# Local and pooled attention with two feed-forward layers: three stages, weights decoded into place, 512-token blocks

## The chip, the cores and the metric

One core of a Trainium2 chip runs the whole program. The time is the device time of one execution in microseconds (us). Data lies in SBUF and matmul results in PSUM (8 banks); TensorE (PE) multiplies, VectorE (DVE), ScalarE (ACT) and GpSimd (POOL) do the elementwise work, and DMA queues of SyncE (SP) and ScalarE move data to and from DRAM.

## The reference

```python
# q, k, v: [4, 8, 576, 64]; pooled attention over means of 4 tokens, repeated 4 times
out_d = sm_attn(mean4(q), mean4(k), mean4(v))           # 144 queries, 144 keys
# local attention: |i - j| < 4
scores = where(mask, 0.125 * q @ k.T, -1e9); out_local = softmax(scores) @ v
x = (repeat(out_d, 4) + out_local) -> [2304, 512]       # tokens, heads * dim
x = ((x @ w_a) * (x @ w_b)) @ w_out                     # 512 -> 1536 -> 512
h = x @ w_in; return (h * clip(h + 3, 0, 6) / 6) @ w_out2   # 512 -> 2048 -> 512
```

The weights arrive as float64. Every matrix product of the two feed-forward layers is done in three passes on operands split into two float32r parts (small terms first, `PASSES`).

## The kernel before, in words

Attention works on units of 116 tokens (5 to a batch, 20 in all; the last of a batch has 112). `local` does half a unit, two head pairs: scores against keys laid out with zeros (`kz`, L306), maximum, exponentials, scaling, a transpose (`turn`) and the product with the values (`pv`), which adds the pooled result and splits the sum into `x`. `pooled` does one head pair of one batch (16 in all): sums over four tokens, 144 x 144 scores, softmax, product.

Weights are decoded by `decode` (L83 to L124): a load of 1 MB into `raw`, five VectorE passes (L102, L103, L104, L107, L109) that turn float64 words into float32, an add (L115, on GpSimd) and a split into two parts (`split`, L79 on ScalarE, L80). The 12 tiles of `wab` go to their places (`wh`). The 6 tiles of `wo` and the 16 of `w2` are written to DRAM (`later_weights`) and read back at the last block (L542, L547).

The first feed-forward layer's hidden part is done in six blocks of 3, 3 and 4 units (348, 344 and 460 tokens), 12 tiles each (`pab`, L523), and stored to DRAM (`h_d`). In the last part, blocks of 256 tokens run `second` (acc, L569) for the next block between `ph` (L601) and `last` (oacc, L591) of the present one.

The order is written as lists of (time, task) in slots of half a tile; a `tick` in the projection loop issues what is due. The compiler's planner then orders each engine's instructions by the order of the program and its own estimate of when operands are ready. An engine takes its instructions in order, and so do the SP and ACT DMA queues.

Of the kernel before, what the change touches and what calls it, by code (L numbers as in the profile page):

```python
# [25 lines left out]
UW = QB + KB             # tokens that a unit sees  # L26
# [5 lines left out]
HL = 2                   # tiles of the hidden layer in a load  # L32
HP = 4                   # head pairs
SCALE = 0.125

# The upper words, read as float32, of the least and the largest weight that float32r holds.
# [3 lines left out]
# (part of the weights, part of the activations): small terms first  # L40
# [3 lines left out]
PAR = {'banks': 1, 'b_draw': 3, 'dec': 'pp pp pv', 'b_eT': 2, 'abufs': 3, 'b_dq': 1, 'b_e': 4, 'early': -5, 'ord0': 4, 'b_dk': 1, 'lead': 3, 'pem': '111', 'ld0': 2, 'means': 'pv pv vv', 'spl': 'vvp', 'th0': 0.5, 'ls2': 2, 'every0': 3, 'cl': 'pppvvv', 'at0': 3, 'tail': 3, 'b_z': 4, 'th1': 1, 'b_dv': 1, 'norm': 'va ap pp', 'm1': 4, 'th2': 1, 'every': 1.7, 'ahead': 3, 'pre': 5, 'cp': 'aa aa aa', 'vs': 'ppp', 'step0': 2.5, 'lead2': 2, 'ahead0': 2, 'b_vraw': 1, 'hq': 'a', 'nab': 4, 'tk': 1, 'nlast': 5, 'b_de': 3, 'b_mx': 2, 'b_xf': 2, 'b_q': 2, 'mexp': '000'}  # L44


@with_exitstack
def fused_kernel(ctx: ExitStack, tc: tile.TileContext, qt, kt, vt, qd, kd, vd, wab, wo, w2, mask, out):
# [9 lines left out]
    wpool = ctx.enter_context(tc.tile_pool(name="wpool", bufs=1))  # L58
    dram = ctx.enter_context(tc.tile_pool(name="dram", bufs=1, space=bass.MemoryType.DRAM))
    ps = ctx.enter_context(tc.tile_pool(name="ps", bufs=1, space=PSUM))  # L60

# [5 lines left out]
    nc.sync.dma_start(mask_sb, mask)  # L67
# [5 lines left out]
    w2_d = dram.tile([F2, P, 2, W], F32, name="w2_d")  # L73
    wo_d = dram.tile([F1 // 2, P, 2, W], F32, name="wo_d")
    h_d = dram.tile([F1, P, NT], F32, name="h_d")

    def split(dst, src, eng):
        """dst[:, 0] + dst[:, 1] == src, each part with 12 significant bits."""
        nc.scalar.activation(dst[:, 0], src, AF.Copy)  # L79
        eng.tensor_tensor(dst[:, 1], src, dst[:, 0], op=ALU.subtract)  # L80

    def decode(pool, src, dst, put=None, add=nc.gpsimd, sub=nc.gpsimd):
        """float64 -> float32, rounded to nearest, in two parts: [load, first part, second part, put]  # L83

        dst(raw) gives tiles [P, 2, n] with n adding up to W, in order."""
        T = {}

        def load():
            T["raw"] = pool.tile([P, W], mybir.dt.uint64, tag="raw", bufs=2, name="raw")
            nc.sync.dma_start(T["raw"], src)  # L90

        def words():
            w = T["raw"].bitcast(U32).rearrange("p (n t) -> p n t", t=2)
            return w[:, :, 0], w[:, :, 1]

        def upper():
            lo, hi = words()
            m = T["m"] = pool.tile([P, W], F32, tag="dm", bufs=2, name="m")
# [5 lines left out]
            nc.vector.scalar_tensor_tensor(out=mu, in0=hi, scalar=0xC0000000, in1=mu,  # L104
                                           op0=ALU.bitwise_and, op1=ALU.bitwise_or)
            # the lower word, on the value's binade
            nc.vector.tensor_scalar(hi, mu, 0xFF800000, None, op0=ALU.bitwise_and)  # L107
            low = lo.bitcast(F32)
            nc.vector.scalar_tensor_tensor(out=low, in0=lo, scalar=2.0 ** -52, in1=hi.bitcast(F32),  # L109
                                           op0=ALU.mult, op1=ALU.mult)  # L110

        def parts():
            lo, _ = words()
            m = T["m"]
            add.tensor_tensor(m, m, lo.bitcast(F32), op=ALU.add)  # L115
            T["dst"] = dst(T["raw"])
            at = 0
            for t in T["dst"]:
                n = t.shape[2]
                split(t, m[:, at:at + n], sub)  # L120
                at += n

        return [load, upper, parts, lambda: put(T["dst"])]

    eng = {"a": "act", "p": nc.gpsimd, "v": nc.vector}
    A = PAR.get
    eng = {"a": "act", "p": nc.gpsimd, "v": nc.vector}
    NORM = [[eng[x] for x in y] for y in A("norm", "aa ap pp").split()]
    MEANS = [[eng[x] for x in y] for y in A("means", "pv pv vv").split()]
    PEM = [x == "1" for x in A("pem", "110")]  # L130
    SPL = [eng[x] for x in A("spl", "ppp")]
    VS = [eng[x] for x in A("vs", "ppp")]
    MEXP = [x == "1" for x in A("mexp", "000")]
    CP = A("cp", "aa aa aa").split()
    CL = [eng[x] for x in A("cl", "pppppv")]
    DEC = [[eng[x] for x in y] for y in A("dec", "pp pp pp").split()]
    STEP, AHEAD, TAIL = A("step", 3.3), A("ahead", 3), A("tail", 2)
    AHEAD0, AT0, EVERY0, PRE = A("ahead0", 3), A("at0", 3), A("every0", 3), A("pre", 3)
    EVERY, FIRST, LEAD, LEAD2 = A("every", 1.6), A("first", 0), A("lead", 3), A("lead2", 4)
    EARLY, ABUFS = A("early", -3), A("abufs", 3)  # L140
    BUFS = {"draw": 3, "vraw": 1, "dq": 1, "dk": 1, "dv": 1, "de": 3, "deT": 3, "dmx": 2, "dz": 4, "od": HP,
            "q": 2, "v": 2, "e": 4, "eT": 3, "xf": 1, "mx": 2, "z": 4}
    for x in BUFS:
        BUFS[x] = A("b_" + x, BUFS[x])

# [4 lines left out]
    place, sizes = {}, []    # of a unit: its block and where it begins there; tokens of a block  # L150
    for m in range(B // 2 * len(NBU)):
        sizes.append(0)
        for _ in range(NBU[m % len(NBU)]):
            u = len(place)
            place[u] = m, sizes[m]
            sizes[m] += unit_tokens(u)
    NBLK = len(sizes)
    begin = [sum(sizes[:m]) for m in range(NBLK)]

    ods = {}  # L160
    xs = {}
    loaded = {}

    class Work:
        """Where a part of the attention has its tiles, and which engines do what."""

        def __init__(self, bufs, tags, kz, vz, norm, means, pemask, spl, vs, mexp, cp):
            self.bufs, self.tags, self.kz, self.vz = bufs, tags, kz, vz
            self.norm, self.dnorm = norm
            self.qsum, self.ksum = means  # L170
            self.pemask, self.spl, self.vs, self.mexp, self.cp = pemask, spl, vs, mexp, cp
            self.n = 0

        def tile(self, shape, tag):
            if isinstance(self.bufs[tag], list):
                t = self.bufs[tag].pop(0)
                self.bufs[tag].append(t)
                names = "abc"[:len(shape) - 1]
                sizes = dict(zip(names, shape[1:]))
                return t[:shape[0]].rearrange(f"p ({' '.join(names)}) -> p {' '.join(names)}", **sizes)  # L180
            pool, n = self.bufs[tag]
            return pool.tile(shape, F32, tag=tag, bufs=n, name=tag)

        def psum(self, shape, name):
            tag, n = self.tags[self.n % len(self.tags)]
            self.n += 1
            return ps.tile(shape, F32, tag=tag, bufs=n, name=name)

    def copy(eng, dst, src):
        if eng == "a":  # L190
            nc.scalar.activation(dst, src, AF.Copy)
        else:
            nc.vector.tensor_copy(dst, src)

    def normalise(eng, e, z, n):
        """e[:, i] *= z[:, i], i < n"""
        if eng == "act":
            for i in range(n):
                nc.scalar.activation(e[:, i], e[:, i], AF.Copy, scale=z[:, i:i + 1])
# [488 lines left out]
```

## Time and profile before

| | |
|---|---|
| median of 3 runs | 1084.3 us (1083.38 to 1085.85) |
| profiled execution, first to last instruction | 1085.6 us |
| TensorE matmuls busy | 1017.6 us, 94% |
| VectorE busy | 576.5 us, 53% |
| ScalarE busy | 421.7 us, 39% |
| GpSimd busy | 245.5 us, 23% |
| DMA | 145.42 MB |

Busy shares are averages over very different stages; the slices and stretches below show which engine fills which stage. The program's first and last instructions bound the span, and no other time of the profiled execution is recorded beside it.

### The profile page before, as it was taken

Reading aid. Unit: us, or ns where it says so; the run is one execution under the profiler, and the core shown is the slowest. Engines: PE = TensorE matmul, PEld = TensorE weight load, DVE = VectorE, ACT = ScalarE, POOL = GpSimd, SP = SyncE. Lnnn points to the kernel's source line nnn. Section 1 sums busy time; section 2 is a strip of 40 time slices with the busy share of each in tenths; the row PEclk is TensorE's granted clock in tenths of the full one; section 3 lists DMA queues with packets and bytes.
Section 4 is the critical chain, followed back from the end, with each engine's and each line's share of the span. In section 5 each row is a group of like instructions: output and inputs, shape, how many; then the busy total and the mean of one; then the engine's idle time right before and its main releaser. Section 6 shows DMA issues by size and latency. Waiting matters only on the chain.

```text
span 1085.6 us, 18160 instructions
## 1 busy us (share of the span) xinstructions
PE 1017.6 (94%) x7080; PEld 917.6 (85%) x7080; DVE 576.5 (53%) x1073; ACT 421.7 (39%) x1208; POOL 245.5 (23%) x188
## 2 busy tenths in 40 slices
PE   3668778999999999999999999999999999999998
PEld 2457657987788799999999999999999999999997
DVE  5999998778898887511233323232333333333232
ACT  4643554444544454311233324242333333333242
POOL 4767664344554734300000000000000000000000
PEclk9999968999999999999999999999999999999999
DMA  9835465777777576596641111111011111101000
GB/s 245 228 113 190 153 208 161 237 260 256 260 258 253 207 269 233 197 408 216 219 189 30 40 31 38 34 35 37 23 49 30 40 30 40 30 21 49 1 21 19
DMA packets 54340, 145.42 MB, mean 134 GB/s; under 512 B 6000, under 2 KB 34160, under 8 KB 44272
## 3 DMA queue, kind: packets, MB, share of 16 engines
q1 hardware_dynamic: 39568, 130.13, 35.4%
q10 hardware_dynamic: 14688, 14.16, 4.5%
q8 instruction: 55, 0.90, 0.3%
q14 instruction: 29, 0.24, 0.1%
HBM read 102.32 MB, written 41.94 MB: 133 GB/s over the span
## 4 chain that ended last, share of the span: by engine, by line
PE 71%; DVE 14%; DMA 8%; issue 3%; ACT 2%; POOL 1%; SPq 0%; ACTq 0%; DVEq 0%; POOLq 0%
PE ph L601 19%; PE oacc L591 18%; PE pab L523 16%; PE acc L569 14%; DVE m L104 2%; DVE raw L107 2%; DMA raw<-w 2%; DVE mx L329 1%; PE sc L206 1%; DVE raw L109 1%; DVE m L102 1%; DVE z L338 1%; DMA raw<-wab 1%; DMA raw<-wo 1%; PE po L206 1%
## 5 line engine op out<-in xcount | busy, mean ns | idle before, releaser
L523 PE MATMUL pab<-x,wh 128*128 128x348 f32 (+2 forms) x1728 | 344.6, 353 | 6.8 <-ACT x L79 3.9
L523 PEld LDWEIGHTS pab<-x,wh 128*128 128x128 f32 x1728 | 300.0, 197 | 28.1 <-issue 8.0
L605 DVE SCALAR_TENSOR_TENSOR r<-r,ph 128x256 f32<-128x256 f32 x144 | 60.7, 421 | 293.9 <-ACT r L604 293.1
L604 ACT ACTIVATE r<-ph,three 128x256 f32<-128x256 f32 x144 | 68.4, 475 | 283.2 <-PE ph L601 282.8
L601 PEld LDWEIGHTS ph<-x,wh 128*128 128x128 f32 x1296 | 169.5, 191 | 8.1
L569 PE MATMUL acc<-h,wo 128*128 128x256 f32 x1296 | 175.6, 283 | 0.0
L601 PE MATMUL ph<-x,wh 128*128 128x256 f32 x1296 | 173.4, 283 | 0.0
L591 PE MATMUL oacc<-wh,g 128*128 128x512 f32 x648 | 167.6, 394 | 0.0
L569 PEld LDWEIGHTS acc<-h,wo 128*128 128x128 f32 x1296 | 165.7, 191 | 0.9
L591 PEld LDWEIGHTS oacc<-wh,g 128*128 128x128 f32 x648 | 114.8, 189 | 18.9
L80 DVE TENSOR_TENSOR g<-r,g 128x256 fp32r<-128x256 f32 x144 | 61.2, 425 | 64.2 <-PE acc L569 35.8
L115 POOL TENSOR_TENSOR m<-m,raw 128x1024 f32<-128x1024 f32 x34 | 83.1, 2445 | 47.0 <-issue 14.0
L79 ACT ACTIVATE g<-r 128x256 fp32r<-128x256 f32 x144 | 59.9, 416 | 60.1 <-DVE r L605 60.1
L528 DVE TENSOR_TENSOR a<-a,pab 128x348 f32<-128x348 f32 (+2 forms) x72 | 39.4, 548 | 53.8 <-PE pab L523 32.5
L336 ACT ACTIVATE e<-sc,mx 128x64 f32<-128x64 f32 x136 | 40.9, 315 | 63.5 <-DVE mx L329 56.1
L80 DVE TENSOR_TENSOR h<-hr,h 128x256 fp32r<-128x256 f32 x108 | 45.8, 425 | 33.5 <-ACT h L79 29.4
L601 PEld LDWEIGHTS ph<-x,w 128*128 128x128 f32 x432 | 56.7, 188 | 3.3
L79 ACT ACTIVATE h<-hr 128x256 fp32r<-128x256 f32 x108 | 44.9, 417 | 33.9 <-PE acc L569 26.8
L601 PE MATMUL ph<-x,w 128*128 128x256 f32 x432 | 57.5, 281 | 0.0
L527 ACT ACTIVATE a<-pab 128x348 f32<-128x348 f32 (+2 forms) x72 | 35.4, 491 | 54.3 <-PE pab L523 53.4
L591 PE MATMUL oacc<-w,g 128*128 128x512 f32 x216 | 54.6, 396 | 0.0
L101 ACT ACTIVATE m<-raw 128x1024 f32<-128x1024 f32 x34 | 39.1, 1151 | 30.5 <-DMA raw<-wab 11.2
(89 smaller groups left out, 1051.4 us busy)
## 6 DMA issues: line engine op xcount, KB each, us to landing
raw<-w SPq DMA_DIRECT2D x16, 1024.0 KB
w_d<-raw SPq DMA_DIRECT2D x16, 1024.0 KB, 3.9
hr<-h_d ACTq DMA_DIRECT2D x54, 256.0 KB, 5.5
raw<-wab SPq DMA_DIRECT2D x12, 1024.0 KB, 4.9
wh<-w_d SPq DMA_DIRECT2D x12, 1024.0 KB, 5.4
raw<-wo SPq DMA_DIRECT2D x6, 1024.0 KB
wo_d<-raw SPq DMA_DIRECT2D x6, 1024.0 KB
wo<-wo_d SPq DMA_DIRECT2D x6, 1024.0 KB
```

The source lines that it names most:

```text
L79: nc.scalar.activation(dst[:, 0], src, AF.Copy)
L80: eng.tensor_tensor(dst[:, 1], src, dst[:, 0], op=ALU.subtract)
L101: nc.scalar.activation(m, hi.bitcast(F32), AF.Abs)
L115: add.tensor_tensor(m, m, lo.bitcast(F32), op=ALU.add)
L336: nc.scalar.activation(e[:, i], masked[:, i], AF.Exp, bias=mx[:, i:i + 1], scale=SCALE, accum_out=z[:, i:i + 1])
L523: nc.tensor.matmul(p_, wab_t[f][:, x, c], xs[n, g // 2][:, g % 2, y, :nb], start=(g == 0 and i == 0), stop=(g == KC - 1 and i == 2))
L528: nc.vector.tensor_tensor(a, a, pab[1], op=ALU.mult)
L569: nc.tensor.matmul(accs[n][e], wo_t[f // 2][:, x, c], hs[n, f][:, y], start=(f == 0 and i == 0), stop=(f == F1 - 1 and i == 2))
L591: nc.tensor.matmul(oacc[e], g_[:, x, e * P:(e + 1) * P], w2_t[f][:, y, DM:], start=(f == 0 and i == 0), stop=(f == F2 - 1 and i == 2))
L601: nc.tensor.matmul(ph, w2_t[f][:, x, g * P:(g + 1) * P], x2s[n, g][:, y], start=(g == 0 and i == 0), stop=(g == KC - 1 and i == 2))
L604: nc.scalar.activation(r, ph, AF.Relu, bias=three)
L605: nc.vector.scalar_tensor_tensor(out=r, in0=r, scalar=6.0, in1=ph, op0=ALU.min, op1=ALU.mult)
```

## The change

The program becomes three stages in sequence: hidden part of the first layer (`job`), its second product (`second`, result x2 to DRAM and back), the second layer (`final`). `second` and `final` use 512-token blocks (four, and one of 256). Blocks of attention and projections are of 3, 2, 3, 3, 3, 3, 3 units, and the first jobs go over blocks 0 and 1 with the first six weight tiles, then tiles 6 to 8 of both, and so on. Weights are decoded on VectorE alone, straight into the place where they are used: `wo` during the last projection block, `w2` during `second` in the slots that `wab` leaves. A local step does all four head pairs of a unit at once, a pooled step all four score tiles; q and k are loaded once per head pair of a batch and serve both kinds of attention. Scores share one pair of PSUM banks (`s2`), but in the first two blocks, which also use the projections' banks.

```diff
-NBU = (3, 3, 4)          # units of a block of the first FFN's hidden layer, over two batches
-NC = 256                 # tokens of a block of what follows
+BLOCKS = (3, 2, 3, 3, 3, 3, 3)
+NC = 512
...
+        def rest():          # decode, all of it after the load
...
+            nc.vector.scalar_tensor_tensor(out=low, in0=lo, scalar=2.0 ** -52, in1=m, op0=ALU.mult, op1=ALU.mult)
+            v = hi.bitcast(F32)
+            nc.vector.tensor_tensor(v, v, low, op=ALU.add)
+            w = put()
+            nc.scalar.activation(w[:, 0], v, AF.Copy)
+            nc.vector.tensor_tensor(w[:, 1], v, w[:, 0], op=ALU.subtract)
...
+    def two_banks(first, name):
+        tag = "s2"
+        if first:
+            tag = start_banks[count[0] % len(start_banks)]      # ["s2", "ab", "ab"]
+            count[0] += 1
+        return ps.tile([P, 2, BANK], F32, tag=tag, bufs=2 if tag == "ab" else 1, name=name)
...
+            src = qks[b, g] = ap.tile([P, 2, WQ], F32, tag="qk", bufs=6, name="qk")
...
+            T["v_"] = ap.tile([HD, 2, FACTOR, P], F32, tag="vraw", bufs=1, name="vraw")
...
+                for i, h in ((0, 0), (1, 1), (0, 1), (1, 0)):      # local scores
+                    nc.tensor.matmul(sc[64 * i:64 * i + 64, h, p * KB:(p + 1) * KB],
+                                     src[r, 0, HALO + c:HALO + c + KB], src[r, 1, c:c + KB],
+                                     start=False, stop=(p == HP - 1))
...
+            scaled(nc.vector if first else nc.gpsimd, e.rearrange("q p h k -> q (p h) k"),
+                   z.rearrange("q p h -> q (p h)"))
...
+    def load_h(n, f):
+        h = hs[n, f] = pools["p2"].tile([P, 2, NC], F32R, tag="hg", bufs=4, name="h")[:, :, :hi - lo]
+        nc.scalar.dma_start(h[:, 1].bitcast(F32), h_d[f][:, lo:hi])
+    def split_h(n, f):
+        nc.scalar.activation(h[:, 0], src, AF.Copy)
+        nc.vector.tensor_tensor(h[:, 1], src, h[:, 0], op=ALU.subtract)
...
+    jobs = [(0, f) for f in range(6)] + [(1, f) for f in range(6)]
+    jobs += [(n, f) for f in range(6, 9) for n in range(2)]
+    jobs += [(2, f) for f in range(9)]
+    jobs += [(n, f) for n in range(3) for f in range(9, F1)]
+    jobs += [(n, f) for n in range(3, NBLK) for f in range(F1)]
...
+    attend([([], *x[1:]) for x in g0], -20, -10, 2.5, 0)
+    attend(groups_of(1, True), 0.5, 2, 1.0, 12)
+    attend(groups_of(2), 6, 13, 1.5, 4)
+    attend(groups_of(3), 22, 31, 2.0, 6)
...
+    at = {f: f - 3 for f in range(6)} | {6: 7, 7: 8.5, 8: 10, 9: 16, 10: 19, 11: 22}
+        put(at[f] - 4 if f > 1 else -84 + f, load)      # wab
+        put(at[f], rest)
...
+        put(T1 + 1.8 * i, load)                         # wo; T1: first job of the last block
+        put(T1 + 1.8 * i + 1, rest)
...
+        put(T2 + k - 3, load_h, n, f)                   # T2: number of jobs
+        put(T2 + k - 1.5, split_h, n, f)
+        put(T2 + k, second, n, f)
...
+        t = T2 + 0.5 + 3.6 * f if f < F1 + 2 else T3 + 0.5 + 1.5 * (f - F1 - 2)     # w2
+        put(t - 3, load)
+        put(t, rest)
```

## Rows read from the trace of the kernel before

**Rows 1.** The page, busy tenths in 40 slices of 27 us.

```profile
PE   3668778999999999999999999999999999999998
DVE  5999998778898887511233323232333333333232
```

**Rows 2.** Stretches: us, busy (x) of PE, PEld, DVE, ACT, POOL, clock, DMA, GB/s.

```profile
0.00:69.70 69.70, 32.73 (x252) 22.56 (x252) 57.59 (x105) 34.89 (x129) 41.69 (x42) 1.00 0.76 212
69.70:185.00 115.30, 94.21 (x624) 81.63 (x625) 111.47 (x146) 54.77 (x179) 75.49 (x42) 0.87 0.51 165
185.00:455.00 270.00, 263.80 (x1993) 230.71 (x1992) 219.17 (x376) 132.19 (x439) 127.66 (x103) 0.98 0.70 244
...
540.00:1082.00 542.00, 541.85 (x3717) 503.69 (x3715) 171.88 (x413) 185.14 (x431) 0.00 (x0) 1.00 0.13 40
```

**Rows 3.** The chain that ended last: start us, us, what; matmuls in unbroken runs.

```profile
415.23 3.97 PE pab L523 x24
...
495.71 2.51 PE pab L523 x12
...
656.08 1.44 PE ph L601 x12
657.52 2.80 PE oacc L591 x12
```

**Rows 4.** Timeline of PE, attention at full clock: start us, us, what.

```profile
237.79 0.72 PE L206 MATMUL dsc<-dk,dq 64*72 64x144 f32 x8
...
243.97 0.66 PE L209 MATMUL dpt<-ident,de 72*72 72x72 f32 x8
...
258.63 0.71 PE L206 MATMUL dpo<-deT,dv 72*64 72x144 f32 x8
...
429.33 0.38 PE L209 MATMUL pt<-ident,e 128*128 128x128 f32 x2
...
435.30 0.68 PE L206 MATMUL po<-eT,vz 128*64 128x58 f32 x16
...
439.80 0.28 PE L206 MATMUL sc<-mask_sb,ident 128*128 128x256 bf16 x1
440.01 0.66 PE L206 MATMUL sc<-kz,q 128*64 128x128 f32 x8
```

**Rows 5.** Timeline of DVE, passes of a decode and a small one between.

```profile
401.09 1.21 DVE L80 TENSOR_TENSOR raw<-m,raw 128x1024 fp32r<-128x1024 f32 x1
402.23 0.68 DVE L102 TENSOR_SCALAR m<-m 128x1024 f32<-128x1024 f32 x1
...
403.84 0.16 DVE L329 TENSOR_SCALAR mx<-mx 128x4 f32<-128x4 f32 x1
403.91 1.21 DVE L104 SCALAR_TENSOR_TENSOR m<-raw,m 128x1024 uint32<-128x1024 uint32 x1
...
406.26 1.22 DVE L109 SCALAR_TENSOR_TENSOR raw<-raw 128x1024 f32<-128x1024 uint32 x1
```

**Rows 6.** Lines of VectorE, a small scaling: xcount | busy us, mean ns | idle before.

```profile
L329 DVE TENSOR_SCALAR mx<-mx 128x4 f32<-128x4 f32 x40 | 32.8, 822 | 0.3
```

**Rows 7.** The same view, sums and maxima of attention.

```profile
L327 DVE TENSOR_REDUCE mx<-sc 128x4 f32<-128x256 f32 x40 | 16.5, 413 | 4.2 <-PE sc L206 4.1
...
L225 DVE TENSOR_REDUCE dk<-draw 128x144 f32<-128x576 f32 x12 | 8.9, 738 | 0.0
```

**Rows 8.** The chain that ended last, at the start.

```profile
9.03 10.10 DMA wh<-qd
```

**Rows 9.** Timeline of PE, the first projection; brackets: idle before, and its releaser.

```profile
69.66 1.24 PE L523 MATMUL pab<-x,wh 128*128 128x348 f32 x3 [3.93 <-ACT x L79]
```

**Rows 10.** DMA issues: count, size, median us from issue to landing.

```profile
hr<-h_d ACTq DMA_DIRECT2D x54, 256.0 KB, 5.5
...
out<-o SPq DMA_DIRECT2D x18, 256.0 KB, 2.0
```

**Rows 11.** Lines of VectorE, the split of a hidden tile.

```profile
L80 DVE TENSOR_TENSOR h<-hr,h 128x256 fp32r<-128x256 f32 x108 | 45.8, 425 | 33.5 <-ACT h L79 29.4
```

More of the change, by code (lines that the diff above doesn't have):

```diff
@@ L134, in fused_kernel @@
[L134 to L142, printed above, removed]
@@ L156, in fused_kernel @@
             sizes[m] += unit_tokens(u)
+    begin = [sum(sizes[:m]) for m in range(len(sizes))]
     NBLK = len(sizes)
[L158 to L199, printed above, removed]
-        else:
-            eng.tensor_tensor(e, e, z.unsqueeze(2).to_broadcast(list(e.shape)), op=ALU.mult)
-    newest = [None]
-    def mm(*args, **kw):
-        newest[0] = nc.tensor.matmul(*args, **kw)
@@ L557, in split_h @@
[L557 to L565 removed]
+            dst = xs[m][:, :, :, at:at + tokens]
+            nc.scalar.activation(dst[:, :, 0], xf[:, :, :tokens], AF.Copy)
@@ new lines, in final, with put @@
+        return hidden, last, end
+    events = []
+    def put(t, task, *args):
+        events.append((t, len(events), task, args))
+    jobs = [(0, f) for f in range(6)] + [(1, f) for f in range(6)]
[3 more added lines that the diff above has]
+    jobs += [(n, f) for n in range(3, NBLK) for f in range(F1)]
+    when = {j: t for t, j in enumerate(jobs)}
+    for j, t in when.items():
+        put(t, job, *j)
@@ new lines, in attend, with groups_of @@
+    def attend(groups, first, last, lag, loads):
+        for i, (load, score, turn, pv) in enumerate(groups):
+            t = first + (last - first) * i / max(1, len(groups) - 1)
+            for x in load:
+                put(t - loads, x)
+            put(t, score)
+            put(t + lag, turn)
+            put(t + 1.6 * lag, pv)
+    def groups_of(m, first=False):
+        res = []
+        for u in (u for u in place if place[u][0] == m):
+            if u % NU == 0:
+                res += [pooled(u // NU, g, first) for g in range(HP)]
+            res.append(local(u, first))
+        return res
@@ new lines, in fused_kernel, with open_p2, open_p3 @@
+    at = {f: f - 3 for f in range(6)} | {6: 7, 7: 8.5, 8: 10, 9: 16, 10: 19, 11: 22}
+    for f in range(F1):
+        load, rest = decode(wab[f], wab_put(f))
+        put(at[f] - 4 if f > 1 else -84 + f, load)
+        put(at[f], rest)
+    T1 = when[NBLK - 1, 0]
+    T2 = len(jobs)
+    def open_p2():
+        actx.close()
+        pools["p2"] = ctx.enter_context(tc.tile_pool(name="p2", bufs=1, reuse_waits="tile"))
+    def open_p3():
+        xctx.close()
+        pools["p3"] = ctx.enter_context(tc.tile_pool(name="p3", bufs=1, side="right", reuse_waits="tile"))
@@ new lines, in fused_kernel @@
+    k = T3
+    put(T3 - 5, load_x2, 0)
+    put(T3 - 2, split_x2, 0)
+    for n in range(len(spans)):
+        hidden, last, end = final(n)
+        for f in range(F2):
+            put(k + f, hidden, f)
+            if f >= 2:
+                put(k + f + 0.1, last, f - 2)
+        if n + 1 < len(spans):
+            put(k + 4, load_x2, n + 1)
+            put(k + 10.2, split_x2, n + 1)
+        put(k + F2 - 0.5, end)
+        k += F2
+    for _, _, task, args in sorted(events, key=lambda x: x[:2]):
+        task(*args)
```

607 lines of the change are left out of this document (237 added, 370 removed).

## The prediction

> **What bounds the kernel now.** I read the page's slices first, then stretches, then the chain. TensorE is near full only from about 175 us on, while VectorE is at 80 to 100% for the first 450 us and near 20 to 30% after it [rows 1]. The stretches say the same in sums: 32.7 of 69.7 us of matmul before the first projection, 94.2 of 115.3 us at a mean clock of 0.87 up to 185 us with VectorE at 111.5, 263.8 of 270 us up to 455 us, and 541.9 of 542 us in the last half [rows 2]. So the second half is bound by the matmuls, and what can be saved is idle TensorE time in the first 185 us, where VectorE is the limit, plus whatever a matmul costs over its columns.
>
> A floor, from steady repeats on the chain [rows 3]: 3.97 us for 24 matmuls of 344 or 348 columns is 0.1654 us each; 2.51 for 12 of 460 is 0.2092; 1.44 for 12 of 256 is 0.1200; 2.80 for 12 of 512 is 0.2333. The projections (pab) are six blocks of 288: 576 x (0.1654 + 0.1654 + 0.2092) = 311.0 us. acc and ph are 1296 + 1728 = 3024 of 256: 362.9 us. oacc is 864 of 512: 201.6 us. Together 875.5 us. Attention on TensorE at full clock [rows 4]: a half unit takes 0.28 + 0.66 + 0.38 + 0.68 = 2.0 us, so 40 of them 80 us; a pooled group 0.72 + 0.66 + 0.71 = 2.1 us, 16 of them 33.4. Total 988.9 us. The profiled span is 1085.6 us (1.3 above the median of 1084.3), so 96.7 us is idle or slow TensorE. Of it some 49 us lie before 69.66 us, the first projection (69.7 less 20.4 of attention), some 37 us between there and 185 (115.3 less 321 projections, 53.1 us, and about 25 of attention), and only about 11 in the 900 us that follow, the tail of 3.7 included. That sum is what the change is weighed against.
>
> **Block sizes.** Seven blocks instead of six, six of 344 to 348 tokens and one of 228. At 0.1654, and 0.106 for 228 columns (the line through the 256- and 344-column rows), stage one costs 1728 x 0.1654 + 288 x 0.106 = 316.4 us, 5.4 more. With 512-token blocks acc and ph are 4 x 336 matmuls of 512 and 336 of 256: 313.6 + 40.3 = 353.9 us, 9.0 less. oacc keeps its 864. Net -3.6 us: 871.9.
>
> One rule would price this differently. By the rows, two matmuls of 256 cost 0.2400 and one of 512 costs 0.2333, so each pair saves 6.7 ns. The Trainium skill (TensorE: Matmul & The Clock Gate, Back-to-back issue gap) gives a constant of about 2.5 ns over the columns; by that the pair would save 2.5 ns and the 512-token blocks 3.4 us instead of 9. The trace has 0.2333 where that formula has 0.216, so the rows decide.
>
> **Attention on TensorE.** Transposes, values and pooled matmuls keep their number. Local scores become 16 of 64 rows per unit instead of 8 of 128 rows with zeros. No row has that shape. Between 32 recorded matmuls at the price of the narrow po matmuls (0.68 / 16 = 0.043, 1.36 us) and half of that if opposite corners of the array run side by side, against 16 x 0.083 = 1.32 now, the bounds over 20 units are +1 and -13 us. I take 0, nearest to the po row: 113.4 us. The new floor is 871.9 + 113.4 = 985.3 us.
>
> **Decoding.** One weight tile takes three one-input passes of 0.68, two two-input passes of 1.21 and a final subtract of 1.21 on VectorE when nothing holds it up [rows 5]; the add, formerly on GpSimd, has the subtract's form, 1.21. Sum 6.9 us, all of it now on VectorE, 34 x 6.9 = 235 us. What changes is when. Before, all 34 run before 455 us. After, 12 fall in the projections, 6 in their last block, 16 in the later stages. The write to DRAM and the read back go: 22 tiles of 1 MB each way, hidden before, so worth nothing by itself.
>
> **The lock between VectorE and GpSimd.** A tiny VectorE scale that takes 0.16 us alone [rows 5] averages 0.82 over 40 of them [rows 6]; the excess, 26 us in this one line, is time in which a GpSimd operation was running. The Trainium skill (GPSIMD Engine Reference, Key points) says that the two share their SBUF interfaces and contend where VectorE runs a two-port mode or takes two SBUF inputs. By that rule the new adds and subtracts would also suffer from what is left on GpSimd, at the most as the first kind does. GpSimd's part falls from 245 us [rows 2] to about 90 by my count (value sums, scalings after block one, small clears), so I take a third of the old waits.
>
> **The start.** Per pooled group VectorE has two sums at 0.74, a maximum at twice 0.41, small ones of about 0.5 and a scaling of about 0.8: 3.6 us. Per unit, with a maximum at twice 0.41, small ones, scaling, the addition and the subtract, also about 3.6 [rows 7]. To reach the first projection it does 4 + 3 of these, 25 us, and, since it has gaps, about two decodes, 14 us. Data arrives at 5 us, and the value tiles have one buffer: each waits for the sum of the one before, queued behind 1 MB weight loads on SP; such a queued load took 10.1 us in the old start [rows 8]. I put the first projection at 48 us (bounds 38, when only the 25 us and one decode count, and 66, when nothing is gained), against 69.66 [rows 9]. The six jobs of block zero then need six decodes: 41 + 25 + 7 for block one's two units + 3 for evacuation = 76 us of VectorE, plus 5 for data and 8 for waits: 89 us. TensorE has by then 20 + 8.4 us of attention and 6 x 24 x 0.1654 = 23.8 us of jobs, 52 in all, so 37 are idle. The blocks interleave from there: up to block two's first job VectorE needs three decodes, 21, attention about 19 and evacuation 5, against some 57 us on TensorE. TensorE is the limit from there on.
>
> **What is left over.** 37 us to 89 us; 5 for half-clock stretches between bursts (0.87 in [rows 2]); 10 for late attention steps, since scores now share one double bank that is held through eight exponentials; 5 in the last projection block, where six decodes (41 us) and 12 evacuations (6 us) meet 48 us of matmul; 6 in the acc stage (below); 2 at its end; 4 tail. Sum 69. 985.3 + 69 = 1054 us. Bounds of the unknowns: -10 for the start alone and -13 for the score matmuls, -10 for stalls that don't come; +18 for the start, +15 for the later stages. That is 1022 to 1087.
>
> **The acc stage, where cover can go.** A step is 12 x 0.2333 = 2.8 us, with a hidden tile loaded to one of four slots, split by ScalarE and VectorE (0.425 on VectorE at 256 columns [rows 11]; about 0.69 at 512, on the line to the 1.21 at 1024). VectorE has 14 decodes and 60 splits, 97 + 38 = 135 of 151 us. The loop of a slot is: matmul 2.8, issue 0.4, load, split 1.4, and any wait on VectorE, against four steps, 11.2. Loads of the old form took 5.5 us in the middle and stores of 2 KB rows 2.0 [rows 10]; both ends leave the loop at 6.6 to 10.1 plus the wait. Waits of one VectorE operation (1.2) fit, a whole decode ahead (5.7) does not.
>
> **Rivals.**
> - *Slot loop binds (slower).* If the split stands behind a decode's six operations every time and the load takes 5.5 us, the loop is 15.8 us, 3.95 a step, and 48 steps lose 55 us: 1109. It makes the kernel slower from a loop of about 13.8 us on (31 us over 48 steps). For it: VectorE at 90%, 1 MB loads beside the small ones. Against: the two-input rows of one decode [rows 5] lie 2.35 us apart, with a one-input pass and smaller operations of other tasks between them, so work of others gets in. Chance 0.13.
> - *VectorE still paces the projections.* If the lock stays as dear and the decodes come at 8 us, block zero ends near 100 us and the next decodes are late too: 20 to 30 us more, 1079. For it: a VectorE chain in the old start; against: a third of GpSimd's load. Chance 0.17.
> - *The start is short and nothing stalls.* First projection at 38 us, score matmuls side by side: 1027. Chance 0.13.
> - *No gain from decoding in place*, if the decodes of w2 are pushed into the last stage, where a decode and two passes of 0.69 (8.3 us) exceed a step of 5.6: 14 x 2.7 = 38 us, 1092. Slots do come free with the last projection block, which speaks against it. Chance 0.04.
>
> **How the numbers follow.** Forecast 1054 with chance 0.53, own range 1035 to 1075. A measurement can tell 0.2%, 2.2 us, from nothing. Faster: nearly all of the forecast, the short start, and three in four of the VectorE case: 0.52 + 0.13 + 0.13 + 0.02 of the rest = 0.80. Same 0.05. Slower 0.15, nearly all from the slot loop and late decodes. Leaving out about one in ten at either end gives 1022 to 1090.
>
> **What would show it.** First projection at 45 to 52 us and the sixth job at 80 to 95; VectorE's decode passes at 0.68 and 1.21; TensorE full from about 100 us with 0.233 us a matmul in acc and ph; acc and ph near 354 us in busy time. Wrong, if acc starts more than 2.85 us apart with waits on the split, if attention on TensorE is far from 113 us, or if projections wait on weights after 100 us.

## The result and the profile after

The changed kernel takes 1089.1 us (median; 1088.2 to 1095.2) where the kernel before takes 1084.3 (1083.1 to 1085.9): a ratio of 1.0058, interval 1.0033 to 1.0082. It is slower by half a per cent, and the forecast was 1054 us. The profiled execution took 1088.15 us, its span is 1086.3. Every profile read below ran at a mean granted clock of 0.96 or more, but that of e9, which ran at 0.574 and took 1630 us, so that none of its stages is read.

The page's slices, which answer to [rows 1]: TensorE now starts as slowly as before and has a dip in the middle and several near the end, where before it was full.

```profile
PE   4548888999999999999899897999899899899998
DVE  6778986152224222578778784222222322222222
```

The same by stretches, columns as in [rows 2], cut at the first projection (71.1), at 185, at the last projection (503.7) and at the last acc (665.7):

```profile
0.00:71.10 71.10, 31.42 (x323) 22.58 (x323) 48.82 (x76) 30.37 (x115) 23.85 (x37) 0.88 0.54 165
71.10:185.00 113.90, 96.25 (x911) 87.38 (x912) 103.10 (x143) 55.26 (x179) 27.86 (x24) 0.89 0.47 155
185.00:503.70 318.70, 315.68 (x2630) 293.93 (x2629) 122.08 (x220) 108.45 (x375) 32.82 (x42) 1.00 0.27 88
503.70:665.70 162.00, 149.56 (x684) 121.68 (x683) 127.73 (x157) 69.00 (x100) 0.00 (x0) 0.96 0.62 201
665.70:1082.00 416.30, 398.04 (x1803) 329.10 (x1801) 109.90 (x168) 114.48 (x189) 0.00 (x0) 0.98 0.06 20
```

The start gained no time: the first projection comes at 71.1 us (69.7 before) and the sixth job ends at 110.7, and TensorE was busy 127.7 of the first 185 us (126.9 before [rows 2]). By then it has done more for that, 447 projection matmuls on record and the attention of eight units instead of 321 and six, since the work became cheaper (below). TensorE's timeline:

```profile
71.07 0.66 PE L331 MATMUL pab<-x,wh 128*128 128x348 f32 x1 [1.28 <-ACT x L314]
...
106.64 4.10 PE L331 MATMUL pab<-x,wh 128*128 128x348 f32 x24 [0.28 <-DVE a L334]
```

The acc stage has 12.4 us without a matmul and a mean clock of 0.96; the last stage 18.3 and 0.98, where the last 542 us before had 0.2 and 1.00.

The work itself became cheaper than forecast. The chain in the last stage, against 2.80 us for 12 matmuls of 512 columns [rows 3]:

```profile
676.81 2.72 PE oacc L421 x12
679.53 2.72 PE ph L405 x12
```

And a unit's attention on TensorE, timeline, against two half units at 0.28 + 0.66 + 0.38 + 0.68 [rows 4]: mask, scores, transposes and products now take 0.39 + 0.69 + 0.60 + 1.15 = 2.83 us instead of 4.0. These are lengths of runs, and the end of one lies over the start of the next (246.83 + 0.39 is past 247.16), so the difference is an upper bound: fewer, longer runs have fewer such ends.

```profile
246.83 0.39 PE L264 MATMUL sc<-mask_sb,ident 128*128 128x256 bf16 x2
247.16 0.69 PE L270 MATMUL sc<-qk 64*64 64x64 f32 x32
...
211.71 0.60 PE L293 MATMUL pt<-ident,e 128*128 128x128 f32 x4
...
216.72 1.15 PE L303 MATMUL po<-eT,vz 128*64 128x58 f32 x32
```

So idle time ate up what a cheaper program saved. Where it lies is read from three places.

**The start.** The chain of waits that ends at the first projection, its longer pieces (start, us, what). From 32 us on it is one loop: GpSimd sums over a value tile (L223, L224), the next value tile is loaded into the one buffer, and so on, four sums in all. The load that waits for the fourth leaves SyncE's queue at 58.04, and the 1 MB weight load behind it at 58.39.

```profile
8.07 10.16 DMA raw<-wab
...
32.25 4.44 POOL vraw L223
...
36.75 1.14 POOL dv L224
37.90 3.59 DMA vraw<-vd
...
43.70 3.68 DMA vraw<-vd
...
50.58 4.12 DMA vraw<-vd
...
58.04 0.30 SPq L191
58.39 5.97 DMA raw<-wab
64.44 1.13 ACT m L102
```

**The acc stage.** ScalarE's and TensorE's timeline around 537 us (in brackets: idle before, and its releaser). The first pass of a w2 decode (L102) stands on ScalarE ahead of the copies that split the hidden tiles (L350), and waits 5.75 us for its 1 MB load. Four splits then come at once, and TensorE has waited.

```profile
537.03 1.12 ACT L102 ACTIVATE m<-raw 128x1024 f32<-128x1024 f32 x1 [5.75 <-DMA raw<-w]
...
539.07 2.18 ACT L350 ACTIVATE h<-h 128x512 fp32r<-128x512 f32 x4
...
539.75 1.22 PE L368 MATMUL acc<-h,wo 128*128 128x512 f32 x2 [2.87 <-ACT h L350]
```

ScalarE's waits in that stage (engine, line, waited for: us, times, longest):

```profile
ACT m L102 <- DMA raw<-w: 43.5, 10, 6.1
```

**The last stage.** At its beginning r (L408) waits for a buffer of the ring `xo`, which r, the results x2 and the results o share; at each of the four block borders o and r crowd on ScalarE.

```profile
670.55 0.69 ACT L408 ACTIVATE r<-ph,three 128x512 f32<-128x512 f32 x1 [3.49 <-DMA x_d<-x2f]
...
761.68 1.57 ACT L429 ACTIVATE o<-oacc 128x512 f32<-128x512 f32 x3 [3.25 <-PE oacc L421]
763.13 0.70 ACT L408 ACTIVATE r<-ph,three 128x512 f32<-128x512 f32 x1
...
764.41 0.69 ACT L408 ACTIVATE r<-ph,three 128x512 f32<-128x512 f32 x1 [0.58 <-DMA out<-o]
764.61 1.65 PE L405 MATMUL ph<-x,wh 128*128 128x512 f32 x3 [3.02 <-DVE r L409]
```

TensorE's waits over both later stages:

```profile
PE ph L405 <- DVE r L409: 17.5, 5, 5.9
PE acc L368 <- ACT h L350: 8.5, 5, 2.9
PE acc L368 <- DVE h L351: 3.4, 4, 2.0
```

### The profile page after: what moved, and what is told of

It is laid out like the page before. It is cut to its first block, busy times and chain, and to the rows that moved or that the text cites. A ratio compares the mean times of both kernels' runs of the same rounds, so it can differ in the third digit from the quotient of the medians.

```text
span 1086.3 us, 15797 instructions
## 1 busy us (share of the span) xinstructions
PE 991.3 (91%) x6344; PEld 854.7 (79%) x6344; DVE 511.6 (47%) x762; ACT 378.2 (35%) x958; POOL 84.5 (8%) x103
## 4 chain that ended last, share of the span: by engine, by line
PE 68%; DMA 14%; DVE 9%; ACT 4%; issue 3%; POOL 1%; SPq 0%; ACTq 0%; DVEq 0%; POOLq 0%
PE pab L331 22%; PE ph L405 19%; PE oacc L421 18%; DMA raw<-w 6%; PE acc L368 4%; DMA raw<-wab 3%; ACT m L102 2%; DVE wh L115 2%; PE po L303 1%; DMA qk<-qk 1%; DMA raw<-wo 1%; DMA vraw<-vd 1%; PE sc L270 1%; DVE m L104 1%; DMA h<-h_d 1%
## 5 line engine op out<-in xcount | busy, mean ns | idle before, releaser
L405 PE MATMUL ph<-x,wh 128*128 128x512 f32 (+1 forms) x720 | 165.4, 379 | 17.9 <-DVE r L409 17.5
L368 PE MATMUL acc<-h,wo 128*128 128x512 f32 (+1 forms) x720 | 159.3, 380 | 12.1 <-ACT h L350 8.5
L409 DVE SCALAR_TENSOR_TENSOR r<-r,ph 128x512 f32<-128x512 f32 (+1 forms) x80 | 50.7, 634 | 250.2 <-ACT r L408 250.2
L405 PEld LDWEIGHTS ph<-x,wh 128*128 128x128 f32 x720 | 130.9, 195 | 45.0 <-DVE r L409 19.5
L408 ACT ACTIVATE r<-ph,three 128x512 f32<-128x512 f32 (+1 forms) x80 | 51.6, 645 | 209.6 <-PE ph L405 204.2
L412 DVE TENSOR_TENSOR g<-r,g 128x512 fp32r<-128x512 f32 (+1 forms) x80 | 51.1, 638 | 46.5 <-ACT g L411 46.2
L102 ACT ACTIVATE m<-raw 128x1024 f32<-128x1024 f32 x34 | 38.9, 1145 | 96.4 <-DMA raw<-w 54.4
L411 ACT ACTIVATE g<-r 128x512 fp32r<-128x512 f32 (+1 forms) x80 | 47.0, 588 | 50.6 <-DVE r L409 50.6
L350 ACT ACTIVATE h<-h 128x512 fp32r<-128x512 f32 (+1 forms) x60 | 34.4, 585 | 45.2 <-DMA h<-h_d 38.6
L110 DVE SCALAR_TENSOR_TENSOR raw<-raw,m 128x1024 f32<-128x1024 uint32 x34 | 43.9, 1292 | 0.6
L105 DVE SCALAR_TENSOR_TENSOR raw<-raw,m 128x1024 uint32<-128x1024 uint32 x34 | 43.5, 1280 | 0.2
L112 DVE TENSOR_TENSOR raw<-raw 128x1024 f32<-128x1024 f32 x34 | 42.4, 1246 | 0.6
L103 DVE TENSOR_SCALAR m<-m 128x1024 f32<-128x1024 f32 x34 | 23.5, 691 | 39.6 <-ACT m L102 39.6
```

What stands on the lines that cost most here:

```text
L105: nc.vector.scalar_tensor_tensor(out=hi, in0=hi, scalar=0xC0000000, in1=mu, op0=ALU.bitwise_and, op1=ALU.bitwise_or)
L368: nc.tensor.matmul(accs[n][e], wo_t[f // 2][:, x, c], hs[n, f][:, y], start=(f == 0 and i == 0), stop=(f == F1 - 1 and i == 2))
L405: nc.tensor.matmul(ph, w2_t[f][:, x, g * P:(g + 1) * P], x2s[n, g // 2][:, g % 2, y], start=(g == 0 and i == 0), stop=(g == KC - 1 and i = ...
L408: nc.scalar.activation(r, ph, AF.Relu, bias=three)
L409: nc.vector.scalar_tensor_tensor(out=r, in0=r, scalar=6.0, in1=ph, op0=ALU.min, op1=ALU.mult)
L411: nc.scalar.activation(g_[:, 0], r, AF.Copy)
```

## The experiments

Stage marks below are read from each trace: first projection, last projection (end of stage one), last acc, last oacc. The changed kernel has 71.1, 503.7, 161.8 for the acc stage and 416.3 for the last, 578.1 for the two together. Ratios are to the kernel before. Each mark is read from one execution, and the end of stage one moves from one to the next: with the same stage one as the changed kernel it came at 505.0, 504.1, 505.7 and 511.1 in e2 to e5, and with e1's stage one at 492.3 to 493.6 in e1, e6, e11 and e13, but at 487.1 in e10. A difference of some 7 us there is not shown by the marks alone.

**e1, the value loop.**

```diff
+    spare = [w_slot() for _ in range(2)]
+            if b == 0:
+                T["v_"] = spare[g // 2][:HD, g % 2].bitcast(F32).rearrange("p (c r d) -> p c r d", c=2, r=FACTOR)
+            else:
+                T["v_"] = ap.tile([HD, 2, FACTOR, P], F32, tag="vraw", bufs=1, name="vraw")
```

> The value tiles of batch 0 lie in two weight places that are filled late, so that none of the four loads waits for the sum of the one before; all else as changed. Theory Q (a load that waits in SP's in-order queue, and what stands in order behind it on ScalarE, paces the start): the waits of the first pooled products for the value sums (13 us of gaps between 24 and 44 us) go, the weight load issued at 58.4 us goes out some 15 us earlier and the ScalarE idle of 7.9 us ahead of it goes; first projection at 50 to 56 us instead of 71, the whole 1068 to 1075. Theory V (VectorE's work paces the start, as the prediction had it): VectorE had some 49 of 71 us busy, so it fills what is freed: first projection no earlier than 60 to 65, the whole 1078 to 1084.

1078.9 us, 0.9939 (0.9905 to 0.9974). First projection 60.7, stage one ends at 493.6, 10 us earlier, the rest as it was. The loop was real, and 10 us of the start. But both numbers are those of theory V, not Q's 50 to 56 and 1068 to 1075: something else paces what is left of the start (e8, e13 and e15 ask what).

**e2 and e3, the loads of w2.** e2 loads every third w2 tile to a third buffer; e3 keeps two and puts ScalarE's first pass behind the last copy of the decode before.

```diff
+            T["raw"] = pools["p3"].tile([P, W], mybir.dt.uint64, tag="raw3", bufs=1, name="raw")   # e2, f % 3 == 2
...
+            with (tc.issue_after(seen[0].ins) if late and seen[0] else ExitStack()):               # e3, late for w2
+                nc.scalar.activation(m, hi.bitcast(F32), AF.Abs)
...
+            seen[0] = nc.scalar.activation(w[:, 0], v, AF.Copy)
```

> Every third tile of w2 is loaded into a third buffer, so a load goes out up to one decode earlier. Theory Q: ScalarE stood idle 54 us in the acc stage in front of the first step of a decode, whose load had not come, with the hidden tiles' loads and splits behind it in its order; with the third buffer at least half of these waits go, the acc stage (161.8 us, 139 of it matmuls) falls to 145 to 152, the whole to 1073 to 1080. Theory V (VectorE at 85 to 90% is what the splits wait for): the stage stays within 3 us of 161.8.

> For the w2 tiles the first ScalarE step of a decode may not stand ahead of the last ScalarE step of the decode before; buffers as changed. Theory Q: the step that waits for a load no longer holds up the step that frees the buffer for the next load; waits shrink but the load still starts only after the buffer is free: acc stage 150 to 157. Theory V: no change, 159 to 165, or longer, as the order takes freedom away.

e2: 1076.0 us, 0.9900 (0.9868 to 0.9932), acc stage 149.3. e3: 1075.2 us, 0.9910 (0.9881 to 0.9940), acc stage 148.8. A buffer more and an order alone give the same, so it was not the load's length but what stood behind the instruction that waited for it. In e3's trace ScalarE no longer waits for w2 loads; it waits where it should, for the hidden tiles:

```profile
ACT h L352 <- DMA h<-h_d: 55.4, 23, 6.5
```

**e4 and e5, the last stage.** e4 gives r its own two buffers and moves the evacuation of a block behind two hidden tiles of the next; e5 does the first alone.

```diff
-            r = pools["p3"].tile([P, NC], F32, tag="xo", bufs=4, name="r")[:, :nb]
+            r = pools["p3"].tile([P, NC], F32, tag="r", bufs=2, name="r")[:, :nb]
-        put(k + F2 - 0.5, end)                                                # e4 alone
+        put(k + F2 + (1.5 if n + 1 < len(spans) else -0.5), end)
```

> In the last stage r has two buffers of its own instead of sharing four with the stored tiles, and the evacuation of a block's sums comes in the program behind the next block's first two hidden tiles. Theory P (ScalarE's order and the shared ring make the gaps of 6.3, three of 3.4 and 2.9 us at the block boundaries, and the half clock after them costs again): the last stage falls from 420.6 us to 395 to 402, the whole to 1065 to 1072. Rival (the two PSUM buffers of ph, or the banks of the sums, are the limit): gaps stay above 2.5 us each, the stage at 415 or more.

> One half of the run before it (e4): the tile r of the last stage gets two buffers of its own, instead of sharing the four of xo with the results x2 and o; the evacuation of a finished block stays where the changed kernel has it. e4 took 25 us out of the last stage (416.3 to 391.0 us). Theory S (two causes: the shared ring at the border of the two stages, where r waits for the store of x2, 6.3 us; and ScalarE's order at the four block borders, where r stands behind the o evacuations, 3.41 x 3 + 2.93): the ring alone gives back about 6 us, last stage 408 to 412 us, the gaps at the block borders stay. Rival T (the ring is everything, since o takes its buffers from it too): last stage 391 to 398 us and the border gaps go.

e4: 1066.9 us, 0.9823 (0.9797 to 0.9850). e5: 1066.4 us, 0.9834 (0.9788 to 0.9880). The last stage is 391.0 us in both, and all border gaps are gone with the ring alone. So theory S fell: the shared ring was the whole cause, and the crowding of o and r on ScalarE, which I had read as a second one, followed from it. e5's last stage (columns as above) is full:

```profile
673.00:1064.00 391.00, 390.31 (x1803) 324.82 (x1802) 108.56 (x166) 113.37 (x187) 0.00 (x0) 1.00 0.07 21
```

**e6, e1 + e3 + e4 together.**

> The three cures together: value tiles of batch 0 in spare weight slots (e1), ScalarE's first pass of a w2 decode behind the last copy of the decode before (e3), r apart and the evacuation of a block put behind two hidden tiles of the next (e4). If the three losses are separate places (theory A), the stage lengths of the single runs stand side by side: stage one ends at about 494 us, the acc stage takes 149, the last 389 to 391, the whole 1033 to 1040 us, 0.953 to 0.96 of before. If they share a cause, for example VectorE, or a faster stage only moves the wait to the next (rival B), the gains overlap: 1050 us or more.

1048.4 us, 0.9678 (0.9638 to 0.9717): first projection 60.5, stage one 492.8, but the later stages 549.6 instead of the 537.9 of the single gains. Neither A nor B: most adds up, some 12 us do not. They are missing in the acc stage, which takes 161.1 us, as long as in the changed kernel, though e3's order is in it. One long wait of ScalarE there is behind a load of x2 that it issues itself and that waits for the store of x2; but e3 alone had the same wait (6.3 us), so it does not explain the loss (e10 and e11 ask what does):

```profile
ACT h L356 <- DMA x_d<-x2f: 6.5, 1, 6.5
```

**e9, e10 and e11, loads that ScalarE issues.** e9 is the changed kernel with the loads of h and x2 issued by GpSimd. e10 is e1 + e3 + e5 with that, e11 the same with the loads of x2 alone.

```diff
-        nc.scalar.dma_start(h[:, 1].bitcast(F32), h_d[f][:, lo:hi])
+        nc.gpsimd.dma_start(h[:, 1].bitcast(F32), h_d[f][:, lo:hi])
-            nc.scalar.dma_start(t[:, :, 1].bitcast(F32), x2_d[2 * k:2 * k + 2, :, lo:hi].rearrange("e p t -> p e t"))
+            nc.gpsimd.dma_start(t[:, :, 1].bitcast(F32), x2_d[2 * k:2 * k + 2, :, lo:hi].rearrange("e p t -> p e t"))
```

> The changed kernel with one edit: the loads of h and of x2 in the two later stages are issued by GpSimd, which has nothing else to do there, and no longer by ScalarE. Theory W (a load that ScalarE issues stands behind a ScalarE instruction that waits for a 1 MB weight load, or for the store of x2, and so comes late): the h loads then come as soon as their buffer is free, the acc stage falls from 161.8 to 148 to 154 us; the last stage stays at 416. Rival X (the copies of the split stand behind that same waiting instruction, so an early load changes nothing): acc stage within 3 us of 161.8.

> Values apart (e1), ScalarE's first pass of a w2 decode in its place (e3), r in buffers of its own (e5), loads of h and x2 issued by GpSimd (e9). In e6, without the last of them, the later stages together took 549.6 us where the single gains summed gave 537.9; the waits there were 6.3 us on a ScalarE copy behind the load of x2, which waits for the store of x2, and seven waits of 0.6 to 2.0 us. Theory W: they go, last projection to last matmul 536 to 543 us, first projection at 60.7, whole 1030 to 1040 us. If what is lost in e6 is VectorE's (busy at 83 to 89% in that stage), it stays: 548 us or more, the whole 1044 or more.

> As e10, but only the loads of x2 are issued by GpSimd, those of h by ScalarE as before. Theory W2 (the one long wait, 6.3 us before the last block of the acc stage, is the x2 load in ScalarE's queue): last projection to last matmul 541 to 545 us, 5 to 8 less than e6's 549.6. If the h loads carry most: 547 to 550.

e9: 1085.0 us, 1.0014 (0.9993 to 1.0034), 4 us less than the changed kernel, with intervals that just touch. Its stages are not read; 4 us lie between W's 8 to 14 and X's nothing. e10: 1035.3 us, 0.9561 (0.9524 to 0.9599), later stages 539.9, as W has it, and the acc stage 149.1. e11: 1046.3 us, 0.9636 (0.9608 to 0.9664), later stages 547.3 (acc stage 158.7): W2 fell, the loads of h carry most of it. So by these runs the loads matter once the splits no longer stand behind a decode (e10 against e11), and little while they do (e9, by its median alone). e10's stages:

```profile
0.00:59.00 59.00, 32.08 (x322) 23.07 (x322) 46.53 (x73) 30.38 (x115) 22.26 (x38) 1.00 0.63 190
59.00:185.00 126.00, 108.07 (x994) 99.56 (x995) 108.17 (x149) 56.28 (x183) 23.25 (x23) 0.93 0.45 148
185.00:487.10 302.10, 298.85 (x2531) 278.18 (x2530) 117.88 (x215) 105.91 (x370) 36.69 (x49) 1.00 0.27 89
487.10:636.20 149.10, 145.95 (x700) 121.19 (x699) 130.28 (x160) 71.39 (x106) 32.55 (x56) 1.00 0.66 219
636.20:1027.00 390.80, 390.11 (x1803) 324.62 (x1801) 111.14 (x168) 113.59 (x185) 5.00 (x7) 1.00 0.07 22
```

**e7, the job order.** Block by block, with the decodes and attention of blocks 1 and 2 moved to match.

```diff
-    jobs = [(0, f) for f in range(6)] + [(1, f) for f in range(6)]
...
+    jobs = [(n, f) for n in range(NBLK) for f in range(F1)]
```

> The L-shaped first jobs undone alone: jobs run block by block, all twelve tiles of wab decoded one after another for block 0, and the attention of blocks 1 and 2 put later to match; all else as in the changed kernel. Theory L (the L shape hides decodes: a decode takes 6.9 us of VectorE and a job of block 0 only 4.0 us of TensorE): block 0's twelve jobs then come at the decodes' pace, 12 x 6.9 = 83 us instead of 48 plus attention between them, TensorE has less to do meanwhile, and stage one ends 15 to 30 us later than 503.7 us. Rival M (what VectorE has to do until all weights are there is the same either way, and TensorE makes up its attention meanwhile): stage one ends within 5 us of 503.7.

1095.8 us, 1.0107 (1.0066 to 1.0149); stage one ends at 509.4, 5.7 us later. That is within the spread of that mark (503.7 to 511.1 with the changed kernel's stage one), and the intervals of the two kernels overlap. Up to 185 us TensorE was busy 121.1 us instead of 127.7, but by the last evacuation before the last projection block, at 444.6 us (441.8 in the changed kernel, up to 444.8 in e2 to e5), that is made up. So L's 15 to 30 us fell, and M holds as far as this can tell: no gain of the L shape is shown.

**e8 and e12, what VectorE does in stage one.** Both on top of e1. e8 leaves out six passes in each of the first six decodes; e12 puts each decode's add back on GpSimd.

```diff
+            if light:                                     # e8, f < 6
+                return finish(hi.bitcast(F32))            # copy and subtract alone
-            nc.vector.tensor_tensor(v, v, low, op=ALU.add)
+            nc.gpsimd.tensor_tensor(v, v, low, op=ALU.add)      # e12
```

> On top of e1 (values apart, first projection at 60.7 us, stage one done at 493.6), the first six decodes leave out the passes from the clamp to the add, three at 0.68 and three at 1.21 us of VectorE each, so the first six weight tiles are wrong numbers; all loads, copies and waits between engines stay. It takes 5.7 us of VectorE out of each of six decodes. Theory D (VectorE still paces the start, after the values): the first projection comes 8 to 12 us earlier (49 to 53 us), and stage one ends 12 to 30 us earlier than 493.6. Rival C (the chain of scores, exponentials, scaling, transposes and products paces it, with VectorE waiting in it): the first projection stays within 3 us of 60.7 and stage one ends within 6 us of 493.6.

> On top of e1 (values apart; stage one ends at 493.6 us, acc stage 160.9), one part of the change undone: the add of each decode goes back to GpSimd, where it took 2.45 us, and VectorE is spared 34 times 1.21 us. Theory D (VectorE's total paces the first 150 us): 12 adds less are 14.5 us, of which a third to a half shows, stage one ends 4 to 8 us earlier. Rival K (the lock: while GpSimd works, VectorE's passes take longer, 1.41 instead of 1.28 and 0.82 instead of 0.69 us in the traces, and a decode gets 1.24 us longer from end to end): stage one ends 0 to 8 us later and the acc stage is no shorter.

e8: 1070.9 us, 0.9881 (0.9838 to 0.9923); the first projection comes at 64.9, not earlier, though VectorE was busy only 38.9 us ahead of it, but stage one ends at 482.2, 11.4 us earlier. e12: 1070.4 us, 0.9864 (0.9826 to 0.9902); first projection 63.3, stage one ends at 485.1, 8.5 us earlier. So work taken off VectorE shortens stage one, as D has it, and does not bring the first projection forward, as C has it, though e8's numbers fit neither quite: 64.9 is 4.2 us late where C allowed 3, and 11.4 is just short of D's 12. The marks alone would not carry this (the spread above), but the medians, 8 us under e1's 1078.9, say the same; e12's interval lies clear of e1's, e8's does not quite. Of the 8.5 us of e12, 4.3 are there by the last evacuation before the last projection block (425.0 instead of 429.3), the rest comes in that block, where the six tiles of `wo` lose their add too. Eighteen adds, some 22 us of VectorE, fall in stage one (twelve by the expectation), and less than half of that shows. The add took 1.93 us on GpSimd (xcount | busy us, mean ns | idle before):

```profile
L112 POOL TENSOR_TENSOR raw<-raw 128x1024 f32<-128x1024 f32 x34 | 65.6, 1930 | 257.1 <-DVE raw L110 201.1 <-issue 27.2 <-ACT a L337 12.9
```

VectorE's passes hardly paid for it: the two-input passes (L105, L110) took 1.23 and 1.26 us (1.23 and 1.22 in e1), the clamp (L103) went from 0.75 to 0.79, the shift (L104) from 0.78 to 0.71. The Trainium skill (GPSIMD Engine Reference, Key points) has the two engines contend when VectorE takes two SBUF inputs; of a further cost by that rule e12's trace shows almost nothing, and its adds cost less than they free.

**e13 and e15, decodes ahead of the first projection.** e13 moves the first six decodes two job slots later in the list, e15 orders the third to sixth behind the copy of x of block 0's last unit.

```diff
-    at = {f: f - 3 for f in range(6)} | {6: 7, 7: 8.5, 8: 10, 9: 16, 10: 19, 11: 22}
+    at = {f: f - 1 for f in range(6)} | {6: 7, 7: 8.5, 8: 10, 9: 16, 10: 19, 11: 22}    # e13
...
+            with (tc.issue_after(seen[0].ins) if late else ExitStack()):    # e15, late for 2 <= f < 6; seen[0] is that copy
+                nc.scalar.activation(m, hi.bitcast(F32), AF.Abs)
```

> On top of e1 (values apart; first projection 60.7 us, stage one done at 493.6): the first six decodes stand two job slots later in the list of tasks (at f - 1 instead of f - 3), so that attention's VectorE work goes ahead of more of them. In e1 VectorE did 3.4 decodes, 25 us of its 52 us of work, before the first projection, where the prediction counted two. Theory F (the decodes placed ahead hold up the first projection): it comes at 46 to 54 us. Whether the kernel gains is another question: if VectorE's total paces stage one (theory D), the jobs wait later instead, and stage one ends within 5 us of 493.6. Rival G (attention's own chain sets the first projection): it stays within 3 us of 60.7.

> On top of e1 (values apart; first projection 60.7 us, stage one done at 493.6): ScalarE's first pass of the third to sixth decode is put behind the copy of x of the last unit of block 0, so that VectorE has done two whole decodes before the first projection, as the prediction counted, instead of 3.4. Theory F (the decodes placed ahead hold up the first projection): 1.4 x 6.9 = 9.7 us less on VectorE, the first projection at 49 to 54 us. Rival G (attention's own chain sets it): within 3 us of 60.7. For the kernel: theory D (VectorE's total paces stage one) has the end of stage one within 5 us of 493.6 either way; if an early first projection is worth its time, as the prediction assumed, stage one ends 7 to 11 us earlier.

e13: 1079.3 us, 0.9952 (0.9933 to 0.9972), first projection 59.8. It moved no decode: VectorE did the same 3.4 ahead, presumably because the planner orders by when operands are ready. So it tells nothing. e15: 1086.8 us, 1.0030 (1.0016 to 1.0045): two decodes ahead, and the first projection at 61.6. F fell, G holds, and stage one even ended 9 us later, at 502.9, outside both guesses for it: decodes put off are missed later (the sixth job was evacuated at 116.2 us, in e1 at 106.3). What e15's chain to the first projection consists of, its longest pieces: loads until 26 us, the queue of small ones and then 1 MB, for which ScalarE's first pass waits with exponentials behind it; then VectorE in nearly unbroken order.

```profile
3.78 12.55 DMA wh<-vd
16.34 9.89 DMA raw<-wab
...
29.91 1.21 DVE raw L107
...
32.51 1.26 DVE dqk L202
33.77 1.13 DVE raw L112
34.90 1.18 DVE z L290
36.08 1.26 DVE dqk L202
...
58.39 0.77 DVE dmx L211
...
59.44 1.55 ACT de L218 x8
60.98 0.60 ACT x L320
```

**e14, e10 with the add on GpSimd.**

> e10 (1035.3 us) with the add of each decode back on GpSimd (e12). Theory D (VectorE's total paces the first 180 us, and the gain stands beside the others): stage one ends 5 to 9 us before e10's 487.1, the rest stays at 536 to 543 us, the whole 1026 to 1031 us. If GpSimd's adds hold up its loads of h, or a decode longer by some 0.7 to 1.2 us holds up the acc stage, the rest grows by 3 us or more and the whole stays within 4 us of 1035.

1028.5 us, 0.9485 (0.9452 to 0.9517), against e10's 0.9561 (0.9524 to 0.9599): faster by about 7 us in the median. But the profiled executions, 1032.2 and 1032.9 us, are alike, stage one ends at 487.8 in e14 and 487.1 in e10, and the later stages take 538.5 and 539.9. So where the 7 us lie is not shown, and the expected place, stage one, has none of them: theory D is not confirmed here. The first projection came at 67.0, 8 us later than in e10, and stage one ended at the same time, so how early the first projection comes does not by itself set that end. It is the fastest version, 5% under the kernel before.

## Why the prediction was wrong, step by step

What failed is the idle time: nothing was put down for the last stage, where waits cost 25.3 us; the acc stage had 6 us with the wrong wait in mind, and waits cost about 13; and the first projection, forecast 22 us earlier, came no earlier. That 1089 us still lies inside the stated 1022 to 1090 is luck: work that was up to 38 us cheaper than priced stood against some 70 us of lost time that was not foreseen.

- **Matmuls: mis-sized, to the good.** "0.2333 each" for 512 columns measured 2.72 / 12 = 0.2267, 2208 of them, 14.6 us less. The Trainium skill (TensorE: Matmul & The Clock Gate, Back-to-back issue gap) has a formula that gives 0.216, still less than this trace has, and a lower figure for a sustained stream, which this trace does not come near.
- **Attention on TensorE, "I take 0", failed in size.** Scores came at the lower bound, 32 in 0.69 us; mask, transposes and products fell too. 2.83 instead of 4.0 us a unit, 20 units: 23 us less by this sum of run lengths, at the most, and outside the bound of 13, which was for the scores alone.
- **"First projection at 48", "sixth job 89", failed.** They came at 71.1 and 110.7. Two terms were wrong. The single value buffer was named, but priced within 8 us for all waits; it is a loop of loads and sums on the path (e1: 10 us). And "data arrives at 5 us" is true of the first tile only: the path stays with loads until 18 us in the changed kernel and about 26 us in e15. The other suspect, 3.4 decodes ahead where "about two" were counted, did not bear out: with two the first projection came no earlier (e15), nor with far lighter ones (e8). What holds it at 59 to 61 us after e1 stays open.
- **"Decode all on VectorE", right in the sum, wrong in what it costs.** The seven operations of a tile took 7.1 us (6.9 said). But the prediction let TensorE be "the limit from there on" after 89 us, and e12 says that VectorE's work still counts: 8.5 us of stage one for one pass moved away. This is the rival "VectorE still paces the projections", in part; it rests on e8 and e12, and e14, where the same edit left stage one as it was, does not confirm it.
- **The lock, "a third of the old waits", right.** The small scaling of [rows 6] went from 0.82 us to 0.19, over 8 columns instead of 4, so in this line nearly all of the wait is gone. In the five passes of a decode that stayed on VectorE, against 0.68 and 1.21 each, the excess in sum fell from 0.9 us a tile to 0.2:

```profile
L277 DVE TENSOR_SCALAR mx<-mx 128x8 f32<-128x8 f32 x20 | 3.8, 191 | 0.3
```

- **"6 in the acc stage", failed in its mechanism.** The slot loop was checked against VectorE; what stood ahead of the split was ScalarE's first pass of a decode waiting for DMA, an instruction that VectorE's sums don't show. So the rival "slot loop binds" had the place, the split of h, with the wrong engine and four times the price. e2 and e3 put it at 12.5 and 13.0 us, e10 at 12.7; but beside e1 and e4 the order alone gave nothing (e6), until the loads of h left ScalarE (e10).
- **"oacc keeps its 864 matmuls" and nothing for the last stage: the largest miss.** r, x2 and o were put in one ring of four; the forecast read the diff's line and asked of it only whether the buffers suffice in the steady state. With buffers of its own for r the stage is 25.3 us shorter (e5).

The sum: e10 takes 16.6 us off stage one, 12.7 off the acc stage and 25.5 off the last, 54.8 of the 55.2 between its span (1031.1) and that of the changed kernel (1086.3). Of the 16.6, e1 alone showed 10; the rest is within the spread of that mark. The forecast less up to 38 (cheaper matmuls and attention) is 1016, so some 15 us in e10 are still lost time that the forecast hadn't. They lie mostly in stage one by exclusion, since the acc stage of e10 has 3.2 us without a matmul and the last 0.7: TensorE is still busy only 140.2 of the first 185 us. How much of it is the first projection, at 59 instead of 48, is not shown (e14), and what would bring it to 48 was not found.

## What to carry to other kernels

When a change lets new tasks share an engine that works in order, or a ring of buffers, list for every instruction that can wait on DMA what stands behind it there; in the acc stage 43.5 us of such waits on ScalarE, busy 69 of 162 us, cost TensorE 13. Give a tile that is used up at once (r) buffers apart from tiles that wait for a store (x2, o): two of its own gave back 25 us here. And price a single-buffered load as a loop, its count times (load + use), not as one wait.

## What the runs showed of the hardware

A gap costs more than its length. After the gap at 761 us (3.02 us between matmuls) TensorE's granted clock was at the lower of its two levels for most of the next 3.7 us: 9 matmuls of 512 columns there, 17 in the 3.7 us after (columns as above).

```profile
764.61:768.30 3.69, 3.69 (x9) 2.98 (x10) 1.98 (x3) 1.64 (x3) 0.00 (x0) 0.54 0.17 62
768.30:772.00 3.70, 3.70 (x17) 3.02 (x17) 1.28 (x2) 1.32 (x2) 0.00 (x0) 1.00 0.00 0
```

So five gaps of 17.5 us in sum (TensorE's waits for r, above) cost 25 us in the last stage. And the 32 small score matmuls of a unit, 64 x 64 on alternating corners of the array, took 0.69 us, some 20 ns each, where before the 8 of half a unit, 128 x 64 with half of the operand zeros, took 0.66 [rows 4].
